# GFNet filter with a gated ReGLU branch on one core: inputs laid out by partition, idle matmuls in the head's waits, first products pass by pass, other due times

## The chip, the cores and the metric

The kernel runs on one core of one Trainium2 chip. The metric is the device time of one execution in microseconds (us); lower is better. Before the change the median of three runs is 416.8 us (415.87 to 417.68).

## The reference

The input x is 2048 rows of 512 numbers. It is normalised by row, and goes two ways: through a two-dimensional Fourier filter, and through a gated feed-forward product with a ReLU gate. The second, through SiLU, gates the first.

```python
xn = _layernorm(x, axis=-1)                       # x: (1, 2048, 512)
X  = rfft2(xn, axes=(-2, -1)) * (w_r + 1j * w_i)  # (2048, 257)
s  = irfft2(X, s=(2048, 512))
gate, up = xn @ W_gate, xn @ W_up                 # (512, 1376) each
h  = gate * (gate > 0) * up
g  = silu(h @ W_down)                             # (1376, 512)
return x + s * g
```

## The kernel before

All work on TensorE (PE) is in float16, with each float32 operand split into a high and a low half: a product is three passes, high x high, high x low and low x high (`PASSES`, line 24). High halves are mostly made by ScalarE (ACT) and low halves by VectorE (DVE), as the rest that the high half leaves.

x is worked on in 8 chunks of two row blocks (128 rows each); two chunks make one of 4 feed-forward blocks of 512 rows. A chunk `c` is loaded (`load_x`, 292), its mean and variance taken on DVE (`stats`, 305; `deviation`, 316, with one square root on ACT), normalised into `xf` (`normalise`, 357), and turned so that the model dimension lies on partitions: chunks 0 and 1 by PE transposes into `head` and from there into `xT` (`turn_row`, 399: ACT writes the high half, DVE the low half), later ones by DMA transposes. In parallel `xf` is folded and split for the Fourier stages (`fold`, `split`, `first_stage`).

The two weight matrices W_gate and W_up are cut by columns into 11 tiles of 128 (the last is 96), in seven groups (`GROUPS`, 22). `load_group` (480) loads a group's two pieces `raw`; `squares` (489, ACT) and a matmul with ones into `sum` (`group_scale`, 499) give a scale `p`; `group_split` (507) writes the high and low halves `wgu`. `product` (661) is twelve matmuls (3 passes x 4 pieces of the model dimension) into `gu`; names read `gu<block>_<tile>_<0 gate, 1 up>`. For block 0 the first three tiles are made in two halves of 256 columns, rows 0 and 1 (chunk 0) first, then rows 2 and 3 (chunk 1). `rectify` (697, ACT) makes `r` from the gate, `hidden` (703) makes `h32` (DVE) and `h16` (ACT and DVE), `down` (720) multiplies by W_down (`wds`) into `dn`, and `gate` (736) applies SiLU.

The Fourier path goes through DRAM twice: `first_stage` writes `A_d`; `fft_chunk` (767) reads it, goes through PE stages y, x, z and v, and writes `C_d`. When all of `C_d` is written, `last_stage` (927) loads `ct` in 64-partition pieces, PE makes `s2` of each chunk, ACT copies it to `zz`, GpSimd (POOL), DVE and ACT unfold it through `ae` and `ye` into `sv`, and `finish` (976) multiplies `sv` by the gate, adds it to a fresh load `xt` of x, and stores it.

The order of all work is set ahead of the run: every piece is a `step` with an engine, a cost, reads, writes and sometimes a due time; `Plan.run` (119) gives the remaining steps due times backward from these and lists the steps on each engine, earliest due first among those that could start. Due times and choices of engine are the tables of lines 33 to 41. Each engine then works its list strictly in order. `keep_busy` (391) puts matmuls on constant data into PE's list, whose result `idle` nobody reads; before the change these are 12 steps of three, all ahead of the first useful one.

DMAs are issued from SP, a few from ACT. Before the change x, W_gate, W_up, W_down and the output lie in DRAM in their natural order. Row p*32 + e*16 + n of x belongs to partition 64*e + p, so that a load of x or a store of the output is two DMAs of 64 partitions each (e = 0 and 1); a piece of W_gate is a 512-byte or 1024-byte run for each of four rows of a partition.

Every instruction is recorded through the helper in line 64, so that all rows of the profile say L64, and tiles are told apart by name.

Of the kernel before, what the change touches and what calls it, by code (L numbers as in the profile page):

```python
# [8 lines left out]
F32 = mybir.dt.float32  # L9
# [5 lines left out]
P = 128  # L15
S, D, F = 2048, 512, 1376
N1, N2 = 64, 32
# [14 lines left out]

T0, DOWN, FIRST, FIRST_STEP, MID, MID_STEP, LAST, LAST_STEP = 10.0, 56.9, 49.0, 16.8, 180.6, 14.5, 265.2, 14.8
LOADS, LOADX, LOADU = [0.5, 0.7, 3.5, None, None, None, None], [-1.2, 1.0], 4.0
FOLDS, FOLD_LEAD, MARGIN = ['DVE', 'DVE', 'DVE', 'DVE', 'DVE', 'DVE', 'DVE', 'DVE'], 18.2, 1.83
HIGH_ACT = {(0, 1), (1, 0), (1, 1), (0, 0)}
NORM, TURN1 = (('DVE', 'DVE'), ('DVE', 'ACT')), 'PE'
YCOST, VCOST, SCOST, MODE = .63, .59, .6, .095
BUSY = 12
HURRY, SLOW, SLOW_TO = -1, 1, 20  # L40
LOWS = [("DVE", "DVE")] * 8
# [10 lines left out]
def fwidth(f):  # L52
    return P if f < TAIL else F - P * TAIL
# [172 lines left out]
def pe(n, m):  # L226
    return n * (m / 2370 + .001)


@with_exitstack  # L230
def kernel(ctx: ExitStack, tc: tile.TileContext, x, wg, wu, wd, wl, ew, sp, c_r, c_d, c_m, c_x, c_s, out):
    nc = tc.nc
    PS = bass.MemoryType.PSUM
    xr, outr = (t[0].rearrange("(p e n) d -> e p n d", p=N1, n=NE) for t in (x, out))
    PE, DVE, ACT, POOL, SP = (InOrder(tc, e) for e in (nc.tensor, nc.vector, nc.scalar, nc.gpsimd, nc.sync))
# [56 lines left out]
    def load_x(c):  # L292
        tile_of(f"x{c}", "k4", [P, 2, D], F32)
        for e in range(2):
            engine, queue = (("SP", SP), ("ACT", ACT))[c == 0 and e]
            for i in range(2) if c == 0 else [None]:
                rows = slice(2 * c, 2 * c + 2) if i is None else slice(i, i + 1)
                to = slice(0, 2) if i is None else slice(i, i + 1)
                step(engine, .6, lambda e=e, queue=queue, rows=rows, to=to: queue.dma_start(T[f"x{c}"][64 * e:64 * e + 64, to], xr[e, :, rows, :]),
                     writes=[(f"x{c}", e, i)], lead=14 if c else None, kb=256 if i is None else 128, lag=2.2, due=(LOADX[c] + (i or 0) * .01) if c < 2 else None)  # L300

    def x_names(c, i):
        return [(f"x{c}", e, None if c else i) for e in range(2)]

# [86 lines left out]
    def keep_busy(n):  # L391

        tile_of("idle", "F", [P, 256], F32)
        w = ones.bitcast(F16)
        for k in range(n):
            step("PE", .43, lambda: [matmul(T["idle"], w[:, 0:P], w, start=True, stop=True) for _ in range(3)],
                 writes=["idle"], due=1. + .43 * k, lead=0.)

    def turn_row(c, i):

        if (c % 2, i) == (0, 0):
            tile_of(f"xT{c // 2}", "xg", [P, 4, 8, P], F16)
# [10 lines left out]
        step("PE", 1., run, reads=[(f"xf{c}", i), "cS"], writes=[(f"head{c}", i)])  # L413
# [66 lines left out]
    def load_group(g):  # L480
        w = sum(fwidth(f) for f in GROUPS[g])
        f0 = GROUPS[g][0] * P
        for i, src in enumerate((wg, wu)):
            tile_of(f"raw{g}_{i}", "k4", [P, 4, 2 * P], F32)
            e, queue = (("SP", SP), ("ACT", ACT))[g == 0 and i]
            step(e, .6, lambda i=i, src=src, queue=queue: queue.dma_start(T[f"raw{g}_{i}"][:, :, :w], src.rearrange("(k p) f -> p k f", p=P)[:, :, f0:f0 + w]),
                 writes=[f"raw{g}_{i}"], lead=12 if g else None, kb=2 * w, lag=2.5, due=LOADS[g])

# [75 lines left out]
    def load_down():  # L564
        n = NFT - 1
        for a, b in ((0, 3), (3, 6), (6, 8), (8, n)):
            step("SP", .6, lambda a=a, b=b: SP.dma_start(wdr[:, a + 1:b + 1, :], wd[a * P:b * P, :].rearrange("(k p) d -> p k d", p=P)),
                 writes=[("wd", f + 1) for f in range(a, b)], lead=22, kb=256 * (b - a))
        step("SP", .6, lambda: SP.dma_start(wdr[:fwidth(n), NFT, :], wd[n * P:, :]), writes=[("wd", NFT)], lead=22, kb=192)

# [90 lines left out]
    def product(c, f, i, rows=slice(0, 4), tag="gu"):  # L661
# [14 lines left out]
        def run():  # L676
# [299 lines left out]
    def finish(c, i, due):  # L976
        n, sn, g = f"xt{c}_{i}", f"sv{c}", f"g{c // 2}"
        j = 2 * (c % 2) + i
        tile_of(n, "k2", [P, D], F32)
        for e in range(2):  # L980
            step("SP", .6, lambda e=e: SP.dma_start(T[n][64 * e:64 * e + 64], xr[e, :, 2 * c + i, :]), reads=[(sn, 2)], writes=[(n, "x", e)], lead=8, kb=128)
        for part, cols in enumerate(columns(c // 2, j)):
# [3 lines left out]
            step("DVE", dve(w), lambda s=s, t=t: DVE.tensor_add(t(), t(), s()), port=True,  # L986
                 reads=[(sn, 3 + i, part), (n, "x", 0), (n, "x", 1)], writes=[(n, part)])
            for e in range(2):
                engine, queue = (("SP", SP), ("ACT", ACT))[e and c == NCH - 1 and i]
                step(engine, .6, lambda t=t, cols=cols, e=e, queue=queue: queue.dma_start(outr[e, :, 2 * c + i, cols], t()[64 * e:64 * e + 64]),  # L990
                     reads=[(n, part)], kb=w // 4, due=due, lag=2.2)

# [189 lines left out]
```

## Time and profile before

| | before |
|---|---|
| median of the runs | 416.8 us |
| lowest and highest | 415.87 and 417.68 us |
| profiled execution: span from first to last instruction | 415.5 us |
| profiled execution: other time | none is given beside the span |
| PE busy | 401.9 us, 97% of the span |
| DVE, ACT, POOL busy | 306.6, 188.3, 45.0 us |
| mean granted clock of PE | 0.985 |
| first matmul of a product (`gu`) | 12.88 us |
| end of the last matmul | 410.78 us |

The rows quoted below come from five views: the page, the waits of one engine, the chain of work that ended last in order of time, the timeline of one engine, and busy times by stretch (windows). In a timeline row stand start, time, engine, line, operation, output<-inputs, partitions x elements and count; the bracket at its end gives the engine's idle time just before, and what ended it. A window row holds the stretch, its length, busy time of the engine (and instructions), granted PE clock, busy share of the DMA engines, and GB/s.

### The profile page before, as it was taken

Reading aid. Unit: us, or ns where it says so; the run is one execution under the profiler, and the core shown is the slowest. Engines: PE = TensorE matmul, PEld = TensorE weight load, DVE = VectorE, ACT = ScalarE, POOL = GpSimd, SP = SyncE. Lnnn points to the kernel's source line nnn. Section 1 sums busy time; section 2 is a strip of 40 time slices with the busy share of each in tenths; the row PEclk is TensorE's granted clock in tenths of the full one; section 3 lists DMA queues with packets and bytes.
Section 4 is the critical chain, followed back from the end, with each engine's and each line's share of the span. In section 5 each row is a group of like instructions: output and inputs, shape, how many; then the busy total and the mean of one; then the engine's idle time right before and its main releaser. Section 6 shows DMA issues by size and latency. Waiting matters only on the chain.

```text
span 415.5 us, 7642 instructions
## 1 busy us (share of the span) xinstructions
PE 401.9 (97%) x2981; PEld 211.3 (51%) x2981; DVE 306.6 (74%) x648; ACT 188.3 (45%) x356; POOL 45.0 (11%) x68
## 2 busy tenths in 40 slices
PE   5799999999999999999999999999999999899995
PEld 4486454544444444545555455556455445444554
DVE  3758999999998897435595977888763337988943
ACT  3869863635444359320454435335414335423311
POOL 0000000000000000002030320330330018201200
PEclk9599999999999999999999999999999999999998
DMA  8992301055324777963005235053302299665614
GB/s 208 338 332 61 89 13 50 11 143 70 83 52 121 157 235 246 219 225 115 2 2 166 49 117 165 3 165 100 119 2 50 52 212 221 154 176 141 165 52 101
DMA packets 41764, 51.72 MB, mean 124 GB/s; under 512 B 16064, under 2 KB 24864, under 8 KB 41728
## 3 DMA queue, kind: packets, MB, share of 16 engines
q1 hardware_dynamic: 40880, 50.59, 45.9%
q10 hardware_dynamic: 848, 0.66, 0.6%
q8 instruction: 23, 0.38, 0.4%
q14 instruction: 13, 0.11, 0.1%
HBM read 35.48 MB, written 12.60 MB: 116 GB/s over the span
## 4 chain that ended last, share of the span: by engine, by line
PE 90%; DMA 5%; DVE 2%; SPq 1%; issue 1%; ACT 0%; DVEq 0%
PE gu L64 51%; PE dn L64 27%; PE z L64 3%; PE xx L64 3%; PE s L64 2%; DMA xt<-in_x 2%; DMA x<-in_x 2%; DMA ct<-C_d 2%; PE y L64 2%; PE v L64 2%; SPq L64 1%; PE dn_3b L64 1%; DVE wgu L64 0%; DVE xT L64 0%; DVE ye L64 0%
## 5 line engine op out<-in xcount | busy, mean ns | idle before, releaser
L64 PE MATMUL gu<-xT,wgu 128*128 128x512 f16 (+1 forms) x1032 | 217.3, 368 | 4.7 <-DVE xT L64 2.0
L64 PEld LDWEIGHTS <-wgu 128*128 128x128 f16 x1032 | 100.8, 99 | 110.6 <-issue 7.6
L64 PE MATMUL dn<-wds,h 128*128 128x512 f16 (+2 forms) x528 | 115.5, 372 | 0.0
L64 PEld LDWEIGHTS <-h 128*128 128x128 f16 (+1 forms) x561 | 53.7, 98 | 58.4 <-issue 2.5
L64 ACT ACTIVATE h<-h 128x512 f16<-128x512 f32 (+1 forms) x44 | 27.7, 629 | 70.7 <-DVE h L64 70.6
L64 DVE TENSOR_TENSOR h<-gu,r 128x512 f32<-128x512 f32 (+2 forms) x52 | 33.6, 646 | 23.3 <-PE gu L64 21.9
L64 POOL TENSOR_TENSOR po<-tt,tt 128x256 f32<-128x256 f32 x16 | 14.8, 926 | 284.3 <-DVE tt L64 236.1
L64 ACT ACTIVATE r<-gu 128x512 f32<-128x512 f32 (+1 forms) x44 | 26.1, 593 | 24.6 <-PE gu L64 24.3
L64 DVE TENSOR_TENSOR h<-h,h 128x512 f16<-128x512 f32 (+1 forms) x44 | 30.0, 690 | 4.5 <-ACT h L64 4.2
L64 POOL TENSOR_TENSOR ae<-zz 128x128 f32<-128x128 f32 (+1 forms) x32 | 18.6, 613 | 61.9 <-ACT zz L64 48.5
L64 DVE SCALAR_TENSOR_TENSOR tt<-xsp,cw,wt 128x512 f32<-128x512 f32 x32 | 25.2, 849 | 0.0
L64 ACT ACTIVATE g<-dn,cdi 128x512 f32<-128x512 f32 (+1 forms) x16 | 10.6, 673 | 25.2 <-PE dn L64 25.1
L64 DVE TENSOR_TENSOR z<-z,z 128x1024 f16<-128x1024 f32 x8 | 9.8, 1222 | 15.4 <-ACT z L64 15.4
L64 DVE TENSOR_TENSOR sv<-sv,g 128x512 f32<-128x512 f32 (+1 forms) x17 | 10.9, 673 | 9.7 <-ACT g L64 9.0
L64 DVE BATCH_NORM_STATS2 st<-x 128x6 f32<-128x512 f32 x16 | 10.9, 683 | 8.3 <-DMA x<-in_x 8.3
L64 PE MATMUL gu<-xT,wgt 128*64 128x256 f16 (+1 forms) x144 | 17.0, 309 | 0.0
L64 DVE TENSOR_TENSOR a<-y,a 128x1024 f16<-128x1024 f32 x8 | 9.7, 1218 | 8.0 <-ACT a L64 8.0
L64 ACT ACTIVATE wgu<-raw 128x512 f16<-128x512 f32 x20 | 12.4, 622 | 6.3 <-DMA raw<-in_wu 6.3
L64 DVE SCALAR_TENSOR_TENSOR wgu<-raw,p,wgu 128x512 f16<-128x512 f32 x20 | 14.5, 746 | 0.5 <-ACT wgu L64 0.4
L64 DVE TENSOR_TENSOR xt<-xt,sv 128x512 f32<-128x512 f32 (+1 forms) x17 | 11.5, 690 | 4.4 <-DMA xt<-in_x 4.4
L64 ACT ACTIVATE xs<-xs 128x1024 f16<-128x1024 f32 x8 | 8.5, 1059 | 12.4 <-DVE xs L64 12.4
L64 PEld LDWEIGHTS <-wgt 128*64 128x64 f16 (+1 forms) x144 | 9.5, 106 | 7.1 <-issue 1.7
(135 smaller groups left out, 423.4 us busy)
## 6 DMA issues: line engine op xcount, KB each, us to landing
A_d<-t SPq DMA_DIRECT2D x16, 256.0 KB, 3.2
rw<-in_wl SPq DMA_DIRECT2D x8, 512.0 KB, 6.0
wt<-in_wl SPq DMA_DIRECT2D x8, 512.0 KB, 4.8
at<-A_d SPq DMA_DIRECT2D x8, 512.0 KB, 4.8
C_d<-t SPq DMA_DIRECT2D x16, 256.0 KB, 3.3
ct<-C_d SPq DMA_DIRECT2D x16, 256.0 KB, 6.4
xt<-in_x SPq DMA_DIRECT2D x32, 128.0 KB, 2.8
out<-xt SPq DMA_DIRECT2D x30, 128.0 KB, 2.3
```

The lines of the kernel that those rows point to most:

```text
L64: return lambda *args, **kw: self.tc.keep_in_program_order(f(*args, **kw))
```

## The change

Five things are changed together; what is computed stays the same.

1. **Layout.** The host hands x over as (128 partitions, 16 row blocks, 512), both weight matrices as one array `w` in which each group's gate piece and up piece are contiguous for each partition, and W_down by partition (with its tail of 96 rows as an array of its own). The output is written in the layout of x, and the host puts it back in order. Loads of x and stores of the output become one DMA of 128 partitions where there were two of 64; weight pieces become one run of 2 KB or 4 KB for each partition.
2. **Queues at the start.** Both pieces of group 0 are issued from ACT, and all of x from SP; before, ACT issued half of chunk 0 and the up piece of group 0.
3. **Idle matmuls.** `BUSY` goes from 12 steps to 60: 9 of three matmuls and 51 of one, with a late due time, so that the planner can put them between useful steps.
4. **First products.** The half products of tile 0 for rows 0 and 1 are issued pass by pass (4 matmuls each, with due times 0.9 us apart), and those of all split tiles run over the pieces within a pass, not over the passes within a piece. A step waits for the halves that it reads.
5. **Tables.** Other due times, loads in another order, both normalisations of chunk 0 on ACT, other high halves on ACT.

```diff
-T0, DOWN, FIRST, FIRST_STEP, MID, MID_STEP, LAST, LAST_STEP = 10.0, 56.9, 49.0, 16.8, 180.6, 14.5, 265.2, 14.8
+T0, DOWN, FIRST, FIRST_STEP, MID, MID_STEP, LAST, LAST_STEP = 5.52, 50.66, 44.31, 17.14, 179.63, 14.68, 274.73, 15.17
...
-HIGH_ACT = {(0, 1), (1, 0), (1, 1), (0, 0)}
-NORM, TURN1 = (('DVE', 'DVE'), ('DVE', 'ACT')), 'PE'
+HIGH_ACT = {(0, 1), (2, 1), (0, 0), (1, 0), (1, 1), (3, 0)}
+NORM, TURN1 = (('ACT', 'ACT'), ('ACT', 'DVE')), 'PE'
...
-BUSY = 12
+BUSY, BUSY_COLD = 60, 9
...
     def load_x(c):
         tile_of(f"x{c}", "k4", [P, 2, D], F32)
-        for e in range(2):
-            engine, queue = (("SP", SP), ("ACT", ACT))[c == 0 and e]
-            for i in range(2) if c == 0 else [None]:
...
-                step(engine, .6, lambda e=e, queue=queue, rows=rows, to=to: queue.dma_start(T[f"x{c}"][64 * e:64 * e + 64, to], xr[e, :, rows, :]),
...
+            step("SP", .6, lambda rows=rows, to=to: SP.dma_start(T[f"x{c}"][:, to], x[:, rows, :]),
...
     def keep_busy(n):
...
-            step("PE", .43, lambda: [matmul(T["idle"], w[:, 0:P], w, start=True, stop=True) for _ in range(3)],
-                 writes=["idle"], due=1. + .43 * k, lead=0.)
+            m = 3 if k < BUSY_COLD else 1
+            at = .43 * min(k, BUSY_COLD) + .11 * max(k - BUSY_COLD, 0)
+            step("PE", (.43, .11)[m == 1], lambda m=m: [matmul(T["idle"], w[:, 0:P], w, start=True, stop=True) for _ in range(m)],
+                 writes=["idle"], due=90., lead=90. - at)
...
     def load_group(g):
...
-            e, queue = (("SP", SP), ("ACT", ACT))[g == 0 and i]
-            step(e, .6, lambda i=i, src=src, queue=queue: queue.dma_start(T[f"raw{g}_{i}"][:, :, :w], src.rearrange("(k p) f -> p k f", p=P)[:, :, f0:f0 + w]),
...
+            e, queue = (("SP", SP), ("ACT", ACT))[g == 0]
+            step(e, .6, lambda i=i, queue=queue: queue.dma_start(T[f"raw{g}_{i}"].rearrange("p k f -> p (k f)"), w_in[:, 8 * f0 + 4 * i * w:8 * f0 + 4 * i * w + 4 * w]),
...
     def product(c, f, i, rows=slice(0, 4), tag="gu"):
...
+        def part(n):
+            h, l = PASSES[n]
+            t, xT = T[name][:, i] if tag == "F" else T[name], T[f"xT{c}"]
+            for k in range(4):
+                matmul(t[:, rows], wgu[g][:, h, i, k, o:o + P], xT[:, rows, l * 4 + k, :], start=k == n == 0, stop=k == 3 and n == 2)
...
+        if len(r) < 4:
+            if rows.start == 0 and f == 0:
+                for n, (h, l) in enumerate(PASSES):
+                    step("PE", pe(4, 256), lambda n=n: part(n), reads=[(f"xT{c}", j, l) for j in r] + [("wgu", f, h, i)], writes=out, due=clock[0] + n * .9)
+                tick(pe(12, 256))
+            else:
+                cost = pe(12, 256)
+                step("PE", cost, lambda: [part(n) for n in range(3)], reads=[(f"xT{c}", j, h) for j in r for h in range(2)] + weights(f, i), writes=out, due=tick(cost))
+            return
...
     def finish(c, i, due):
...
-        for e in range(2):
-            step("SP", .6, lambda e=e: SP.dma_start(T[n][64 * e:64 * e + 64], xr[e, :, 2 * c + i, :]), reads=[(sn, 2)], writes=[(n, "x", e)], lead=8, kb=128)
+        step("SP", .6, lambda: SP.dma_start(T[n], x[:, 2 * c + i, :]), reads=[(sn, 2)], writes=[(n, "x")], lead=8, kb=256)
...
-            for e in range(2):
-                engine, queue = (("SP", SP), ("ACT", ACT))[e and c == NCH - 1 and i]
...
+            step("SP", .6, lambda t=t, cols=cols: SP.dma_start(out[:, 2 * c + i, cols], t()), reads=[(n, part)], kb=w // 2, due=due, lag=2.2)
```

What the planner makes of this is seen in the order of the instructions. PE's list around the first products, before (`sum0` and `sum1` are the scale matmuls of groups 0 and 1, `head0` the transposes of chunk 0):

```order
L64 MATMUL idle_111<-ones_93 128x256
L64 MATMUL sum0_188<-m0_173,ones_93 128x2
L64 MATMUL head0_196<-cS_75,xf0_190 128x128 x8
L64 MATMUL sum1_217<-m1_186,ones_93 128x2
L64 LDWEIGHTS wgu0_76
L64 MATMUL gu0_0_0_229<-xT0_214,wgu0_76 128x256
```

and in the changed kernel, from the end of the idle matmuls behind `sum1` to the first product:

```order
L64 MATMUL idle_111<-ones_93 128x256
L64 MATMUL head0_248<-cS_75,xf0_234 128x128 x4
L64 LDWEIGHTS ones_93
L64 MATMUL idle_111<-ones_93 128x256
L64 MATMUL head0_248<-cS_75,xf0_234 128x128 x4
...
L64 LDWEIGHTS wgu0_76
L64 MATMUL gu0_0_0_273<-xT0_264,wgu0_76 128x256
```

In the changed kernel 46 idle matmuls stand ahead of `sum0`, 20 between `sum0` and `sum1`, 9 between `sum1` and the transposes, one between the two rows' transposes and two behind them; before, 36 stand ahead of `sum0` and none behind. The product's first four matmuls are followed there by four of the up half and then by eight more of the gate half.

ACT's list in the same place, before:

```order
L64 ACTIVATE wgu0_76,m0_173<-raw0_1_126 128x512
L64 ACTIVATE q0_171<-q0_171 128x2
L64 ACTIVATE wgu0_76,m0_173<-raw0_0_131 128x512
L64 ACTIVATE wgu1_77,m1_186<-raw1_0_139 128x512
L64 ACTIVATE wgu1_77,m1_186<-raw1_1_144 128x512
L64 ACTIVATE wgu0_76<-raw0_0_131,p0_201 128x512
L64 ACTIVATE xT0_214<-head0_196 128x512 x2
```

and in the changed kernel (rows with `m0` or `m1` are squares, those with `p0` high halves, `q0` is the square root):

```order
L64 ACTIVATE wgu0_76,m0_154<-raw0_0_115 128x512
L64 ACTIVATE wgu0_76,m0_154<-raw0_1_122 128x512
L64 ACTIVATE wgu1_77,m1_195<-raw1_0_131 128x512
L64 ACTIVATE q0_206<-q0_206 128x2
L64 ACTIVATE wgu1_77,m1_195<-raw1_1_139 128x512
L64 ACTIVATE wgu0_76<-raw0_0_115,p0_197 128x512
L64 ACTIVATE xf0_234<-x0_120,q0_206 128x512 x2
L64 ACTIVATE wgu0_76<-raw0_1_122,p0_197 128x512
L64 ACTIVATE xT0_264<-head0_248 128x512 x2
```

Group 0's squares now come first, and the two normalisations of chunk 0 (`xf0`) are in ACT's list where they were in DVE's.

Far behind, in the last Fourier stage, ACT's list puts `r3_5` (which frees the PSUM of product `gu3_5_0`) behind the copy into `sv1` before:

```order
L64 ACTIVATE ye3_4235<-zz3_4214 128x2
L64 ACTIVATE zz4_4237<-s2_4_4187,cwi_88 128x1024
L64 ACTIVATE ae4_4257<-zz4_4237 128x2 x2
L64 ACTIVATE ye4_4260<-zz4_4237 128x2
L64 ACTIVATE sv1_4264<-ye1_4143 128x4
L64 ACTIVATE r3_5_4266<-gu3_5_0_4216 128x512
L64 ACTIVATE h16_3_4_4270<-h32_3_4_4185 128x512
```

and in the changed kernel ahead of it:

```order
L64 ACTIVATE ye2_4227<-zz2_4194 128x2
L64 ACTIVATE r3_5_4229<-gu3_5_0_4169 128x512
L64 ACTIVATE zz3_4245<-s2_3_4198,cwi_88 128x1024
L64 ACTIVATE ae3_4250<-zz3_4245 128x2 x2
L64 ACTIVATE ye3_4254<-zz3_4245 128x2
L64 ACTIVATE h16_3_4_4257<-h32_3_4_4162 128x512
L64 ACTIVATE ye1_4192<-ae1_4189 128x2
L64 ACTIVATE sv1_4279<-ye1_4192 128x4
```

The copy into `sv1` needs `ye1` from DVE, where `ye1` stands in both kernels behind the two additions into `xt0_0` and `xt0_1`. On SP the loads of `xt0` stand in both kernels behind twelve loads of `ct`; they are four DMAs before and two now.

More of the change, by code (lines that the diff above doesn't have):

```diff
@@ L230, with kernel @@
 @with_exitstack
-def kernel(ctx: ExitStack, tc: tile.TileContext, x, wg, wu, wd, wl, ew, sp, c_r, c_d, c_m, c_x, c_s, out):
+def kernel(ctx: ExitStack, tc: tile.TileContext, x, w_in, wd, wd_tail, wl, ew, sp, c_r, c_d, c_m, c_x, c_s, out):
     nc = tc.nc
     PS = bass.MemoryType.PSUM
-    xr, outr = (t[0].rearrange("(p e n) d -> e p n d", p=N1, n=NE) for t in (x, out))
     PE, DVE, ACT, POOL, SP = (InOrder(tc, e) for e in (nc.tensor, nc.vector, nc.scalar, nc.gpsimd, nc.sync))
@@ L293, in load_x @@
         tile_of(f"x{c}", "k4", [P, 2, D], F32)
[L294 to L300 removed]
+        for i in range(2) if c == 0 else [None]:
+            rows = slice(2 * c, 2 * c + 2) if i is None else slice(i, i + 1)
+            to = slice(0, 2) if i is None else slice(i, i + 1)
+            step("SP", .6, lambda rows=rows, to=to: SP.dma_start(T[f"x{c}"][:, to], x[:, rows, :]),
+                 writes=[(f"x{c}", i)], lead=14 if c else None, kb=512 if i is None else 256, lag=2.2, due=(LOADX[c] + (i or 0) * .01) if c < 2 else None)
     def x_names(c, i):
[L303 removed]
+        return [(f"x{c}", None if c else i)]
     def stats(c, q, j):
@@ L412, in run @@
                 PE.transpose(head()[:, cols], T[f"xf{c}"][:, i, cols], cS[:, 7:])
-        step("PE", 1., run, reads=[(f"xf{c}", i), "cS"], writes=[(f"head{c}", i)])
+        step("PE", .5, run, reads=[(f"xf{c}", i), "cS"], writes=[(f"head{c}", i)])
         step("ACT", act(512), lambda: ACT.activation(xt(0), head(), AF.Copy), reads=[(f"head{c}", i)], writes=[(f"xT{c // 2}", j, 0)])
@@ L482, in load_group @@
         f0 = GROUPS[g][0] * P
-        for i, src in enumerate((wg, wu)):
-            tile_of(f"raw{g}_{i}", "k4", [P, 4, 2 * P], F32)
-            e, queue = (("SP", SP), ("ACT", ACT))[g == 0 and i]
-            step(e, .6, lambda i=i, src=src, queue=queue: queue.dma_start(T[f"raw{g}_{i}"][:, :, :w], src.rearrange("(k p) f -> p k f", p=P)[:, :, f0:f0 + w]),
-                 writes=[f"raw{g}_{i}"], lead=12 if g else None, kb=2 * w, lag=2.5, due=LOADS[g])
+        for i in range(2):
+            tile_of(f"raw{g}_{i}", "k4", [P, 4, w], F32)
+            e, queue = (("SP", SP), ("ACT", ACT))[g == 0]
+            step(e, .6, lambda i=i, queue=queue: queue.dma_start(T[f"raw{g}_{i}"].rearrange("p k f -> p (k f)"), w_in[:, 8 * f0 + 4 * i * w:8 * f0 + 4 * i * w + 4 * w]),
+                 writes=[f"raw{g}_{i}"], lead=12 if g else None, kb=2 * w, lag=2.2, due=LOADS[g])
     def squares(g):
@@ L690, in run @@
                     n += 1
-        r = range(*rows.indices(4))
+        def part(n):
[3 more added lines that the diff above has]
+                matmul(t[:, rows], wgu[g][:, h, i, k, o:o + P], xT[:, rows, l * 4 + k, :], start=k == n == 0, stop=k == 3 and n == 2)
+        r = range(*rows.indices(4))
+        out = [(name, j // 2, i) for j in r if j % 2 == 0]
+        sums[c, f, i] = (lambda: T[name][:, i] if tag == "F" else T[name]), [(name, k, i) for k in range(2)]
+        if len(r) < 4:
[7 more added lines that the diff above has]
+            return
         cost = 1.33 if f == TAIL and i == 1 else pe(12, 128 * len(r))
         step("PE", cost, run, mode=3 * (f == TAIL and i == 1), reads=[(f"xT{c}", j, h) for j in r for h in range(2)] + weights(f, i),
-             writes=[(name, j // 2, i) for j in r if j % 2 == 0], due=tick(cost))
-        sums[c, f, i] = (lambda: T[name][:, i] if tag == "F" else T[name]), [(name, k, i) for k in range(2)]
+             writes=out, due=tick(cost))
     def rectify(c, f):
@@ L986, in finish @@
             step("DVE", dve(w), lambda s=s, t=t: DVE.tensor_add(t(), t(), s()), port=True,
[L987 to L991 removed]
+                 reads=[(sn, 3 + i, part), (n, "x")], writes=[(n, part)])
+            step("SP", .6, lambda t=t, cols=cols: SP.dma_start(out[:, 2 * c + i, cols], t()), reads=[(n, part)], kb=w // 2, due=due, lag=2.2)
     step("SP", .6, lambda: SP.dma_start(cR, c_r), writes=["cR"], lead=20, kb=256)
```

21 lines of the change are left out of this document (13 added, 8 removed).

## The prediction

> **What bounds the kernel now.** First the page: who is busy, and the granted clock in 40 slices.
>
> ```profile
> span 415.5 us, 7642 instructions
> PE 401.9 (97%) x2981; PEld 211.3 (51%) x2981; DVE 306.6 (74%) x648; ACT 188.3 (45%) x356; POOL 45.0 (11%) x68
> PEclk9599999999999999999999999999999999999998
> ```
>
> PE is busy for 97% of the span, and the change takes no useful matmul away. So it can only gain where PE waits or runs at a low clock; the second slice, about 10 to 21 us, is the only long one at half clock. Next PE's waits:
>
> ```profile
> PE sum L64 <- ACT wgu L64: 2.7, 1, 2.7
> PE gu L64 <- DVE xT L64: 2.0, 1, 2.0
> PE gu L64 <- ACT r L64: 1.6, 1, 1.6
> ```
>
> The first two lie ahead of the products or in the first. The chain in order of time tells why, and where the third stands (start, length, what):
>
> ```profile
> 4.86 7.45 DMA x<-in_x
> 12.40 0.70 DVE st L64
> 13.89 1.30 DVE xT L64 x2
> 15.23 6.74 PE gu L64 x35
> 23.14 1.46 DVE wgu L64 x3
> 24.65 7.91 PE gu L64 x70
> ...
> 343.89 7.71 DMA xt<-in_x
> 354.61 2.75 PE gu L64 x12
> ...
> 410.80 0.48 ACT g L64
> ```
>
> The second chunk of x, 7.45 us on its way, holds the statistics on DVE, and these stand in DVE's list ahead of the low halves of `xT`, for which PE waits until 15.23. Then 35 matmuls take 6.74 us, 193 ns each; from 24.65 on 70 take 7.91, 113 ns each. From there PE waits once, for 1.6 us before 354.61, for `r` on ACT, which stands behind work that hangs on the loads `xt`. From 354.61 nothing but PE is on the chain until the last SiLU.
>
> The clock, by stretches that fit its steps (PE busy, granted clock, DMA share, GB/s):
>
> ```profile
> 1.05:3.84 2.79, 2.79 (x14) 1.00 0.60 160
> 3.84:6.50 2.66, 2.66 (x24) 1.00 0.95 223
> ...
> 7.25:10.67 3.42, 1.05 (x8) 1.00 1.12 274
> ...
> 14.08:17.49 3.41, 2.26 (x11) 0.50 1.07 365
> 17.49:20.91 3.42, 3.42 (x18) 0.50 1.06 377
> 20.91:24.32 3.41, 3.41 (x34) 1.00 1.08 364
> ```
>
> (For 1.05 to 3.84 no grant is recorded yet; 199 ns for each of the idle matmuls, against 111 ns behind 3.84, says it was half.) The clock is lost at the end of a stretch with PE busy 1.05 of 3.42 us, and comes back only after a stretch filled completely.
>
> **The change, part by part.**
>
> *Loads.* Rates of stretches in which nearly all packets are of one kind, 512-byte pieces of weights first, then 2 KB rows of W_down; and DVE's wait for the first row of x:
>
> ```profile
> 6.50:9.00 2.50, 1.00 1.16 314
> 17.00:19.00 2.00, 0.50 1.04 386
> ...
> 4.47 0.69 DVE L64 BATCH_NORM_STATS2 st<-x 128x6 f32<-128x512 f32 x1 [3.46 <-DMA x<-in_x]
> 7.77 0.63 ACT L64 ACTIVATE wgu<-raw 128x512 f16<-128x512 f32 x1 [5.54 <-DMA raw<-in_wu]
> ```
>
> Now the first 1 MB is group 0 and both rows of chunk 0 (four DMAs of 256 KB, two from each queue). One row has landed by 4.47 before; the other 0.79 MB take 2.0 to 2.5 us at 386 to 314 GB/s, so all have landed by 6.5 to 7.0, where the first weight piece landed at 7.77 before. [...]
>
> *Scale of group 0.* A square takes 0.63 (row above) and up to 0.8 with the read-out of its sum, so the last is done between 7.3 and 7.8. But `sum0` now queues behind 46 idle matmuls: 14 by 3.84, 32 at 111 ns, to 7.4. So `sum0` stands at about 7.6; before:
>
> ```profile
> 9.25 0.38 PE L64 MATMUL sum<-m,ones 128*128 128x2 f32 x2 [2.74 <-ACT wgu L64]
> 10.00 1.43 PE L64 MATMUL head<-cS,xf 128*128 128x128 f32 x8 [0.37 <-DVE xf L64]
> 23.26 1.04 PE L64 MATMUL head<-cS,xf 128*128 128x128 f32 x8
> ```
>
> *From there to the first product.* These rows price the steps: DVE's scale of a group, the deviation with its square root on ACT between, ACT's normalisation, both high halves of `xT`:
>
> ```profile
> 22.12 0.16 DVE L64 TENSOR_SCALAR p<-sum 128x2 f32<-128x2 f32 x1 [2.48 <-PE sum L64]
> 22.32 0.37 DVE L64 TENSOR_SCALAR p<-p 128x2 int32<-128x2 int32 x2
> 17.70 0.17 DVE L64 TENSOR_SCALAR q<-mv 128x2 f32<-128x2 f32 x1
> 19.21 0.16 DVE L64 SCALAR_TENSOR_TENSOR q<-mv,q 128x2 f32<-128x2 f32 x1
> 19.40 0.82 ACT L64 ACTIVATE xf<-x,q 128x512 f32<-128x512 f32 x1
> 11.77 1.06 ACT L64 ACTIVATE xT<-head 128x512 f16<-128x512 f32 x2
> ```
>
> `sum0` 7.6, done 8.0; scale 0.6 to 8.6; deviation 1.67 (17.70 to 19.37) to 10.3, since `q0` now queues behind `p0` on DVE; two normalisations on ACT, the first done at 11.1, the second at 11.9 (before, DVE did both while ACT made squares); ACT's other high half, at the square's 0.63, to 12.5; high halves of `xT` 1.06 to 13.5. PE starts there. Its first eight matmuls need high halves alone (0.9 us). The low halves follow on DVE, which first does `p1` (`sum1`, behind 20 idle matmuls, at 10.2; 0.3 and 0.6 to 11.2), a low half of weights (0.7) and both statistics of chunk 1 (0.70 and 0.2 each; its load, now one DMA of 128 partitions on a faster stream, no longer holds them), to 13.8. Two low halves at 1.30: 15.1 to 15.2.
>
> So PE runs on from 15.2, as before from 15.23, but with 8 of the first 48 matmuls done and at full clock. The other 40 take 4.5 us at 113 ns, the `sum2` among them 0.3, the transposes 1.04: the third product starts at 21.0. Before it started at 24.65. **Gain 3.6 us**, of it some 2.3 from the clock (29 matmuls from 15.23 to 20.91, 80 ns each), the rest from the eight matmuls done early and the wait for `wgu` from 24.3 (23.26 and 1.04) to 24.65. That wait may come back: `sum2` stands behind 24 of the matmuls, at 17.9, `p2` at 18.2; from there to the last split DVE took 2.5 us before (22.12 to 24.6), so 20.7. The margin is 0.3; without it at most the 0.4 of before is lost.
>
> *Idle matmuls and the clock's phase.* When the clock is released is not in the kernel's hands: 2.8 us after PE began in one place, 5.7 in the other (15.23 to 20.91). If it comes 3.4 us later, 17 more idle matmuls cost 88 ns each ahead of `sum0`: between 0 and 1.5 us lost. I take the middle, **0.8 us back**. The idle matmuls between `sum0`, `sum1` and the transposes (20 and 9, 2.2 and 1.0 us) end about when their successors are ready, and cost nothing.
>
> *Late wait.* DVE and SP there:
>
> ```profile
> 349.50 0.72 DVE L64 TENSOR_TENSOR xt<-xt,sv 128x512 f32<-128x512 f32 x1 [0.92 <-DMA xt<-in_x]
> 351.72 0.97 DVE L64 TENSOR_TENSOR xt<-xt,sv 128x512 f32<-128x512 f32 x1 [1.50 <-DMA xt<-in_x]
> 332.05 7.78 SPq L64 DMA_DIRECT2D ct<-C_d x12
> 340.46 3.89 SPq L64 DMA_DIRECT2D xt<-in_x x4
> ```
>
> Behind twelve `ct` loads SP issues four `xt` loads 1.1 us apart (340.46 to the chain's 343.89), since each waits for an earlier DMA; two are left, so that the second row is issued some 2.2 us earlier and `xt0_1` is added by about 350.3 instead of 352.4 (times of before). Also `r3_5` no longer queues behind `sv1`. What is late next: `h32_3_5` on DVE, behind `xt0_1` and two halves of `ye1`; by the 0.72 for 512 columns about 1.4 us later, 351.7. PE came to its wait at 353.0 (354.61 less 1.6) and comes to this one no earlier. So **1.6 us gained**; between 0 and 1.6 if the loads don't come sooner.
>
> *Hidden.* Twice fewer `x`, `xt` and `out` DMAs on SP: SP is waited for nowhere else. A PE that runs 3.6 us ahead needs splits and folds sooner: DVE's and ACT's own waits for loads (3.46 and 5.54 us in the rows above, and the chain's 7.45) shrink with it; if they did not, up to 3.6 would be given back. The tail behind PE, 4.7 us from 410.78 to the end of the span, keeps its steps; its last store is one DMA instead of two on two queues, which I cost at nothing.
>
> **Sum.** -3.6 + 0.8 - 1.6 = -4.4 us on the span of 415.5: 411.1. The median of the runs lies 1.3 above that span, and I keep that: **412.4 us**.
>
> **Rivals.**
>
> *The clock falls anyway in the head.* Between the last long run of idle matmuls and 15.2 PE does 8 transposes, 3 idle matmuls and 8 of the product: some 2.2 of 3.4 us. At 1.05 of 3.42 the clock was lost, at 2.26 of 3.41 it was not given back. If it falls, the 2.3 go: 414.7. For it: that gap in the evidence; against: the idle matmuls run right up to the transposes. [...] Chance 0.10.
>
> *A wait takes the place of the late one*, since DVE's list there is as full as before: 1.6 stays, 414.0. Chance 0.12.
>
> *Slower: the additions of x bind the last stage.*
>
> ```profile
> 354.60:372.50 17.90, 16.23 (x30) 1.00 0.71 183
> DMA to landing us min/median/max: 2.2/2.6/8.4
> ```
>
> DVE is 91% busy there (first row), some 0.65 us spare for a chunk of about 7 (two products at the chain's 2.75, a down step and an `s2`). On SP the `xt` loads of a chunk now stand behind both stores of the chunk before, so they are issued only when DVE has done it. DVE has about 4.3 us of other work until it needs them (four instructions of 512 columns at 0.72 and four of half the width), the loads two or three issues and 2.6 us (second row, median). If landing took 2 us longer, five chunks would lose some 1.3 each, 6.5 in all, and the kernel ends at 418.9; that is the point from which it is slower. For it: 8.4 as the longest; against: that was behind twelve `ct` loads, and a load is now one DMA of 128 partitions. Chance 0.05.
>
> *It doesn't do what it says*: idle matmuls hold up `sum0` by as much as the loads gain, and no late gain: -3.6 + 1.5 + 0.4 = -1.7, 415.1. Chance 0.06.
>
> **Numbers.** About 0.5%, 2.1 us, is what a measurement can tell from no change: faster is below 414.7, slower above 418.9. My forecast, 411 to 414, has 0.67, and with the 0.12 of the late wait and a share of the borders 0.81 for faster; 0.14 for the same (first and last rival, less that share), 0.05 for slower. The range holds the forecast, the late wait and both rivals near 415: 410.6 (1.0 better in the head, no phase cost) to 415.3.
>
> **What would show it.** Right: granted clock 1.00 without a gap from about 4 us; first `gu` at 13 to 14.5; the third product near 21; no wait of PE of 1 us from there to the end. Wrong: half clock in 10 to 21; `sum0` after 9; PE waits for ACT `r` or DVE `h` near 350; DVE waits for `xt` chunk after chunk.

## The result, and the profile after

| | before | changed |
|---|---|---|
| median of four runs (lowest to highest) | 417.24 us (415.87 to 418.29) | **410.87 us** (410.83 to 410.96) |
| profiled execution's span | 415.5 us | 409.1 us (its run took 410.83) |
| mean granted clock | 0.985 | 0.997 |
| third product starts | 24.65 us | 20.05 us |
| span less that start | 390.85 us | 389.05 us |

The changed kernel takes 0.9844 of the time before (95% interval 0.9817 to 0.9871), 6.4 us less. It was run again beside the experiments, and there it gave 411.4 us; why those two differ is part of what follows.

The page of the changed kernel, first the busy times and then the clock:

```profile
span 409.1 us, 7662 instructions
PE 402.5 (98%) x3023; PEld 213.4 (52%) x3023; DVE 306.6 (75%) x646; ACT 190.0 (46%) x359; POOL 47.6 (12%) x68
PEclk9999999999999999999999999999999999999998
```

The slice at half clock is gone, and PE is busy 98% of a shorter span. The whole list of PE's waits:

```profile
PE idle L64 <- DVE md L64: 1.1, 1, 1.1
PE gu L64 <- ACT xT L64: 1.0, 1, 1.0
PE gu L64 <- DVE xT L64: 0.3, 1, 0.3
```

The waits for `sum` (2.7 us before) and for `r` (1.6) are no longer there. PE's timeline in the head:

```profile
1.05 6.69 PE L64 MATMUL idle<-ones 128*128 128x256 f16 x46 [1.05 <-DVE md L64]
7.58 0.28 PE L64 MATMUL sum<-m,ones 128*128 128x2 f32 x2
...
13.35 1.03 PE L64 MATMUL gu<-xT,wgu 128*128 128x256 f16 x8 [0.96 <-ACT xT L64]
14.67 2.78 PE L64 MATMUL gu<-xT,wgu 128*128 128x256 f16 x24 [0.29 <-DVE xT L64]
...
19.17 1.04 PE L64 MATMUL head<-cS,xf 128*128 128x128 f32 x8
20.05 2.13 PE L64 MATMUL gu<-xT,wgu 128*128 128x256 f16 x18
```

`sum0` stands right behind the idle matmuls, the eight high-half matmuls run at 13.35, the low halves come at 14.67, and the third product (last row) starts at 20.05. Before, the chain in order of time began with SP's issues (0.73 to 4.81) and the load of `x` behind them (4.86, 7.45 us). Now its first long piece is this:

```profile
1.05 6.69 PE idle L64 x46
```

The idle matmuls themselves now begin the chain, so they have become a part of what sets the end. The load of chunk 1 no longer does: SP issues it at 3.07 as one DMA, where the first of its two halves went out at 4.30 behind six other issues, and DVE takes the statistics of its first row without a wait (before, at 12.40, behind a wait for the load):

```profile
11.38 0.69 DVE L64 BATCH_NORM_STATS2 st<-x 128x6 f32<-128x512 f32 x1
```

In the table the gain splits at the third product: 4.6 us ahead of it, 1.8 behind it, together 6.4. Behind it, the late wait's 1.6 and 0.4 of the tail (4.7 us from the last SiLU at 410.80 to the end before, 4.3 from 404.83 now) make 2.0; some 0.2 was lost elsewhere.

The clock, by stretches that fit its steps (PE busy, granted clock, DMA share, GB/s):

```profile
4.15:7.56 3.41, 3.41 (x33) 1.00 1.03 368
7.56:10.98 3.42, 3.42 (x35) 1.00 1.03 403
10.98:14.39 3.41, 2.44 (x21) 1.00 1.04 425
```

In the trace full clock is granted at 4.15 us, and from there to the tail it is never lost, the window with PE's wait in it (2.44 of 3.41) included. The DMAs move 368 to 425 GB/s in these windows; before they moved 274 to 377 in the windows from 7.25 to 24.32.

That the part behind the head is nearly constant makes the experiments easy to read: in the eight profiles of the changed kernel and its variants in which PE waits nowhere behind the head, span less start of the third product comes out at 388.9 to 389.1, so a kernel's head can be read from one row.

### The profile page after: what moved, and what is told of

It is laid out like the page before. It is cut to its first block, busy times and chain, and to the rows that moved or that the text cites. A ratio compares the mean times of both kernels' runs of the same rounds, so it can differ in the third digit from the quotient of the medians.

```text
span 409.1 us, 7662 instructions
## 1 busy us (share of the span) xinstructions
PE 402.5 (98%) x3023; PEld 213.4 (52%) x3023; DVE 306.6 (75%) x646; ACT 190.0 (46%) x359; POOL 47.6 (12%) x68
## 4 chain that ended last, share of the span: by engine, by line
PE 98%; DVE 0%; ACT 0%; issue 0%
PE gu L64 55%; PE dn L64 27%; PE s L64 3%; PE z L64 3%; PE xx L64 3%; PE idle L64 2%; PE y L64 2%; PE v L64 2%; PE dn_3b L64 1%; PE head L64 0%; ACT xT L64 0%; PE sum L64 0%; DVE xT L64 0%; ACT g L64 0%; DVE sv L64 0%
## 5 line engine op out<-in xcount | busy, mean ns | idle before, releaser
L64 PE MATMUL gu<-xT,wgu 128*128 128x512 f16 (+1 forms) x1032 | 214.8, 364 | 1.2 <-ACT xT L64 1.0
L64 PEld LDWEIGHTS <-wgu 128*128 128x128 f16 x1032 | 99.4, 98 | 105.0 <-issue 4.6
L64 POOL TENSOR_TENSOR ae<-zz 128x128 f32<-128x128 f32 (+1 forms) x32 | 21.3, 698 | 62.5 <-ACT zz L64 43.2
L64 DVE TENSOR_TENSOR sv<-sv,g 128x512 f32<-128x512 f32 (+1 forms) x17 | 11.8, 722 | 7.5 <-ACT g L64 6.9
```

The costliest lines, as they stand in the source:

```text
L64: return lambda *args, **kw: self.tc.keep_in_program_order(f(*args, **kw))
```

## The experiments

All but two keep the order of every engine as it was, and edit what one step issues; so a difference belongs to the edit. Times are medians of four to twelve runs, on four chips. The kernel before ran beside each of them and took 416.76 to 417.23 us, so a difference of half a microsecond between runs on different chips is not told from none. The ratios in brackets are to before on the same chip, with their 95% intervals.

**The changed kernel again.**

> The changed kernel once more, as the measure for the others. Its first four runs lay at 410.8 to 411.0 us, with the 46 idle matmuls done in 6.69 us; in the runs that differ only behind the head or in the weights' pieces they took 7.28 and 7.31 us and the time was 411.5 to 411.7 us. If the moment at which the clock comes is chance: 410.8 to 411.8 us here, and the span is 389.0 us more than the start of the third product. If the 0.6 us were the price of those edits: 410.9 us again.

411.40 us (410.64 to 412.12). In its profile the 46 idle matmuls take 7.38 us and everything up to the third product (20.74) shifts with them; span 409.7, less 20.74 gives 388.96:

```profile
1.05 7.38 PE L64 MATMUL idle<-ones 128*128 128x256 f16 x46 [1.05 <-DVE md L64]
8.27 0.28 PE L64 MATMUL sum<-m,ones 128*128 128x2 f32 x2
...
20.74 5.51 PE L64 MATMUL gu<-xT,wgu 128*128 128x256 f16 x49
```

So it is chance: the five runs here, all on one chip, reach from below the first four to 1.2 us above them. In the traces full clock is granted at 4.15 us in the first profile of the changed kernel, at 5.57 here, and anywhere from 3.78 to 7.04 in the others, a spread of 3.3 us, about one window of 3.41 us. Here 1.42 us later cost 0.69. The first four runs, which differ by 0.13 us, were probably all early ones (only one of them left a trace), and 411.4 is the better measure for what follows.

**Idle matmuls alone, in the kernel before.**

```diff
+            if g == 0:
+                idle(24)
             matmul(T[f"sum{g}"][:, :2 * nf], ones, T[f"m{g}"][:, :2 * nf], start=True, stop=True)
+            if g < 2:
+                idle((3, 9)[g])
...
+                    if (c, f, i, n) == (0, 0, 0, 1) and rows.start == 0:
+                        idle(20)
```

> The kernel before, every instruction in its old place, with 56 idle matmuls put into PE's waits of the head (24 ahead of sum0, 3 behind it, 9 behind sum1, 20 behind the first matmul of the first product). If the clock is the main part of the head's gain: granted clock 1.00 from about 4 us on, the 35 matmuls from 15.2 take about 4.0 us instead of 6.7, and of these 2.7 us all but the 0.4 of the wait for wgu stays: about 414.5 us, with runs closer together than 415.9 to 418.3. If the gain lies in the layout and the loads: no change, 416 to 418 us.

415.01 us (ratio 0.9941, 0.9921 to 0.9961): 2.2 us faster, and the clock stays. The 35 matmuls of the first product:

```profile
15.53 3.98 PE L64 MATMUL gu<-xT,wgu 128*128 128x256 f16 x35
```

3.98 us against 6.74. The nine runs lie within 2.2 us (413.92 to 416.11), the twenty of before beside them within 4.7 (415.34 to 420.07). So they are closer together, as was expected, though they are fewer; the 2.2 us that are left come from something else than losing the clock. PE's late wait for `r`, in the old order and with loads in halves, is only 0.45 us here (ahead of the product at 351.20).

**The changed kernel without the added idle matmuls.**

```diff
-BUSY, BUSY_COLD = 60, 9
+BUSY, BUSY_COLD = 12, 12
```

> The changed kernel with the 36 idle matmuls of before and no others; the order of all else is the same. If the clock is the main part: it is lost near 10 us and comes back only after a stretch filled by PE, some 20 to 35 matmuls at 80 ns more, 2 to 3 us; sum0 comes about 0.9 us earlier since no idle matmul stands ahead of it: 412.0 to 413.2 us. If the layout is the main part: 410.0 us, the 0.9 gained and nothing lost.

411.95 us (0.9863, 0.9832 to 0.9893), just below the first expectation, and only 0.5 above the changed kernel's second measurement, the control from here on. The two ranges overlap (411.42 to 412.77 and 410.64 to 412.12) and the chips differ, so the 0.5 is not shown by itself. PE by clock window:

```profile
5.99:9.40 3.41, 1.83 (x18) 1.00 1.03 401
9.40:12.82 3.42, 1.54 (x10) 1.00 1.04 417
12.82:16.23 3.41, 3.13 (x15) 0.50 1.01 413
16.23:19.64 3.41, 3.41 (x34) 1.00 1.03 417
```

The clock is lost after a window with PE busy 1.54 of 3.42 us, but comes back after one window, not three as before, since the products now fill it. That window holds 15 matmuls where full ones hold 33 to 35: the price is about 1.4 us (15 at 96 ns more than the 113 of a full one), and `sum0`, with fewer idle matmuls ahead of it (7.39, against 8.27 in the control), returns 0.9. In the new order the idle matmuls are worth little, some 0.5 us by these numbers.

**Layout alone, in the kernel before**, as in the change's layout hunks, with the old tables, product and idle matmuls:

```diff
-queue.dma_start(T[f"x{c}"][64 * e:64 * e + 64, to], xr[e, :, rows, :])
+None if e else queue.dma_start(T[f"x{c}"][:, to], x[:, rows, :])
...
-SP.dma_start(T[n][64 * e:64 * e + 64], xr[e, :, 2 * c + i, :])
+None if e else SP.dma_start(T[n], x[:, 2 * c + i, :])
```

> The kernel before with x, weights, W_down and result laid out by partition, x, xt and out each as one DMA of 128 partitions; the order of every engine, the product and the idle matmuls are those of before. If layout and clock add up to the whole (clock alone brought 2.2 us in this order): about 4 us faster than before, 413 us, with the late wait of PE gone and the first product about 1.5 us earlier, and half clock in a part of the head. If the layout works only together with the new order, which asks for its loads at other times: 415 us or more, with the late wait still there.

413.61 us (0.9913, 0.9890 to 0.9936): 3.6 us faster. The six runs fall into two groups, 412.26 to 412.94 and 414.28 to 414.41, and the profile is one of the second. All of `x` is issued from SP here, as in the change. PE gets its low halves at 13.04, 2.2 us sooner than the kernel before and 1.6 sooner than the changed one. The clock is lost from 11.98 to 18.81. And the late wait is there, though each `xt` is one DMA:

```profile
13.04 6.79 PE L64 MATMUL gu<-xT,wgu 128*128 128x256 f16 x35 [1.11 <-DVE xT L64]
...
352.08 2.75 PE L64 MATMUL gu<-xT,wgu 128*128 128x512 f16 x12 [1.19 <-ACT r L64]
```

**Layout and idle matmuls, in the kernel before** (`idle(8)` ahead of `sum0`, 3 and 14 behind `sum0` and `sum1`, 10 behind the first matmul, added to the last one).

> The kernel before with the new layout (as in the run with layout alone) and 35 idle matmuls in PE's waits of the head; order, due times and product are those of before. If clock and layout add up: the 35 matmuls from 13.0 take 4.0 instead of 6.8 us, the third product starts near 20, the late wait of 0.4 to 1.2 us stays: 411.0 to 412.3 us, so that of the change's 6.3 us only about 1 is left for the new order and the passes. If the new order is needed for the head (the splits of group 2 late on DVE): third product after 21, 412.5 us or more.

411.82 us (0.9877, 0.9855 to 0.9898), with 411.40 for the changed kernel on the same chip. Its head is the shorter one, even with the clock as late as 7.04; the late wait gives that back:

```profile
12.98 3.98 PE L64 MATMUL gu<-xT,wgu 128*128 128x256 f16 x35
...
19.13 7.11 PE L64 MATMUL gu<-xT,wgu 128*128 128x256 f16 x60
...
349.74 2.75 PE L64 MATMUL gu<-xT,wgu 128*128 128x512 f16 x12 [1.51 <-ACT r L64]
```

So layout and idle matmuls make 4.9 of the 5.4 us seen on this chip; new tables and passes add 0.4, which is less than the control's own spread and not shown by these medians. By the profiles, they lose 1.6 in the head (20.74 less 19.13) and gain 2.0 behind it (390.97 less 388.96).

**Weights in 512-byte pieces (1 KB for groups of two tiles), in the changed kernel.**

```diff
-queue.dma_start(T[f"raw{g}_{i}"].rearrange("p k f -> p (k f)"), w_in[:, 8 * f0 + 4 * i * w:8 * f0 + 4 * i * w + 4 * w])
+queue.dma_start(T[f"raw{g}_{i}"], (wg, wu)[i].rearrange("(k p) f -> p k f", p=P)[:, :, f0:f0 + w])
```

> The changed kernel with the gate and up weights read from their old place in pieces of 512 bytes (1 KB for the groups of two); x stays laid out by partition and the order is the same. If pieces of 512 bytes cost rate (314 against 386 GB/s in the trace of before): the weights of groups 0 and 1 land 0.3 to 0.8 us later; the first lie under the idle matmuls ahead of sum0, the second hold ACT's squares ahead of the normalisation, so the first product starts about 0.5 us later: 411.4 us. If pieces of 512 bytes run at full rate: 410.9 us.

411.53 us, the same as the control. The rate is lower, 320 against 420 GB/s from 9 to 12 us (the run without the added idle matmuls, on the same chip as this one, shows 417 from 9.40 to 12.82), and ACT's first two squares start 1.05 and 1.2 us later. Window and ACT's rows in this kernel:

```profile
9.00:12.00 3.00, 3.00 (x31) 1.00 1.15 320
```

```profile
5.36 0.63 ACT L64 ACTIVATE wgu<-raw 128x512 f16<-128x512 f32 x1 [3.14 <-DMA raw<-in_wg]
6.88 0.63 ACT L64 ACTIVATE wgu<-raw 128x512 f16<-128x512 f32 x1 [0.79 <-DMA raw<-in_wu]
```

and in the control:

```profile
9.00:12.00 3.00, 3.00 (x31) 1.00 1.05 420
```

```profile
4.31 0.63 ACT L64 ACTIVATE wgu<-raw 128x512 f16<-128x512 f32 x1 [2.08 <-DMA raw<-in_w]
5.67 0.63 ACT L64 ACTIVATE wgu<-raw 128x512 f16<-128x512 f32 x1 [0.64 <-DMA raw<-in_w]
```

But `sum0` stands behind the idle matmuls until 8.2 anyway. In the changed kernel the weights' layout is hidden under them; what the layout brings there is x's part.

**All x transfers in halves, in the changed kernel.**

```diff
-SP.dma_start(T[n], x[:, 2 * c + i, :])
+[SP.dma_start(T[n][e:e + 64], x[e:e + 64, 2 * c + i, :]) for e in (0, 64)]
```

and likewise for the loads of `x` and the stores.

> The changed kernel with every x, xt and out transfer as two DMAs of 64 partitions each on the same queue, in the same order. If the late wait went because the xt loads are fewer DMAs and so issued sooner: a wait of PE of 1 to 1.6 us near 350 is back, and the rows of x land later in the head, 0.3 to 1 us on the first product: 412.5 to 413.5 us. If it went because r3_5 no longer stands behind the work that waits for xt: no wait near 350, and at most 0.5 us in the head: 411.0 to 411.4 us.

416.08 us (0.9970, 0.9949 to 0.9991): nearly all of the gain is gone, beyond both expectations. The third product starts at 21.29, and span less that is 392.9: 3.9 us are lost behind the head. PE has no wait near 350; its waits lie further on in the last stage. PE's rows there:

```profile
381.06 1.04 PE L64 MATMUL dn<-wds,h 128*128 128x512 f16 x4 [1.21 <-DVE h L64]
382.86 1.50 PE L64 MATMUL gu<-xT,wgt 128*64 128x256 f16 x24 [0.76 <-DVE h L64]
388.65 4.01 PE L64 MATMUL dn<-wds,h 128*128 128x512 f16 x16 [0.38 <-DVE h L64]
```

These three make 2.35 of the 3.9. Some 0.8 more lies in the same stretch, where weight loads wait for `h` too (0.88, 0.53 and 0.49 us from 388.65 to 390.33), and 0.7 in the tail: from the last SiLU (409.23) to the end are 4.97 us, against 4.27 in the changed kernel. DVE's waits for `xt` (us in total, times, longest):

```profile
DVE xt L64 <- DMA xt<-in_x: 5.2, 7, 2.1
```

and SP's rows of one chunk:

```profile
357.13 2.43 SPq L64 DMA_DIRECT2D out<-xt  x4
359.62 2.51 SPq L64 DMA_DIRECT2D xt<-in_x  x4
```

SP's two rows of a chunk in the changed kernel:

```profile
355.40 0.94 SPq L64 DMA_DIRECT2D out<-xt  x2
356.47 0.89 SPq L64 DMA_DIRECT2D xt<-in_x  x2
```

Eight issues of some 0.6 us each keep SP 4.9 us per chunk, four of some 0.45 keep it 1.8. DVE then waits for `xt` (2.3 us and once in the changed kernel), falls behind, and PE waits for `h`.

**Only the late loads, and only the stores, in halves.**

> The changed kernel with only the late xt loads as two DMAs of 64 partitions each; x in the head and the stores stay whole. With everything in halves the kernel took 416.1 us, 1.2 us of it in the head and some 3.9 in the last stage, where DVE waited for xt chunk after chunk. If that comes from the number of issues that stand on SP ahead of a load (four xt of 0.62 us, behind four stores of 0.60): half the surplus goes with the stores, about 1.2 us of 2.4 in a chunk, and with some 0.7 us spare in a chunk little is left: 411.0 to 412.5 us. If it comes from loads of 64 partitions being slow in themselves: 414 us or more.

411.68 us: span 409.7 less 20.67 is 389.03, so nothing is lost behind the head, and no late wait.

> The changed kernel with only the stores as two DMAs of 64 partitions each. With loads and stores in halves the last stage lost 3.9 us, with the loads alone in halves nothing. If it is the number of issues on SP between one chunk's stores and the next chunk's loads (eight in halves 4.9 us; four stores and two loads about 3.3 us, less than the 3.6 us of two stores and four loads that lost nothing): no wait of PE behind the head, the span 389.0 us more than the start of the third product, 410.6 to 411.8 us. If a store in halves is itself the slow part: PE waits for h in the last stage, 413 us or more.

413.55 us (412.74 to 414.88): the second case came out, not the first. Span 411.0 less 19.87 is 391.1, 2.1 lost. Half lies behind PE: from the last SiLU (405.68) to the end are 5.3 us, 1.05 more than in the changed kernel. Of this, 0.8 is the last store, whose two issues keep SP for 1.11 us where one took 0.33. The other half lies on PE, of which one row shows 0.38; behind it weight loads wait for `h` (0.53 and 0.49 us, at 385.96 and 386.78):

```profile
385.11 4.01 PE L64 MATMUL dn<-wds,h 128*128 128x512 f16 x16 [0.38 <-DVE h L64]
```

So it isn't the count of issues alone: this kernel has no more than the one before it. DVE now waits 0.38 and 0.32 us for the second row of two chunks. The stores stand ahead of the loads in SP's list, but that doesn't explain it: counted from the start of the third product, the loads of the first of these chunks have all been issued by 332.4 us here, and by 332.9 in the run before, where DVE doesn't wait for them. Why they come late here stays open. The loss with both in halves, 3.9, is more than the 0 and 2.1 of each alone; that DVE's slack can be used up only once would fit, but is not shown.

**First products not pass by pass.**

```diff
-lambda n=n: part(n)
+lambda n=n: [part(m) for m in range(3)] if n == 2 else None
```

> The changed kernel with the first two products not taken pass by pass: the twelve matmuls of each stand together where its third pass stood; the order of all else is the same. PE then waits from 12.4 for the low halves at 14.6 and starts 8 matmuls of 0.11 us later than they could: 0.9 us, 411.8 us. If the 2.2 us in which PE does nothing cost the clock as well, some 2 us more: 413 to 414 us.

411.99 us; from `sum0` to the third product 12.90 us against 12.47 in the control: the passes are worth 0.43 by the profiles, half of what was expected; the medians, on different chips, can't tell it. The gate half's four high-half matmuls still ran early; only the up half's four moved. The clock stayed (34 matmuls fill the 3.41 us from 15.98).

**Nine idle matmuls fewer ahead of `sum0`** (the steps of `keep_busy` with `k` from 9 to 17 issue nothing).

> The changed kernel with 37 idle matmuls ahead of sum0 instead of 46, all else in its order. sum0 stood at 7.58 while its squares were done at 6.4. If sum0 and the scale behind it set the first product: sum0 at 6.6, the first product 0.9 us earlier, 410.0 us. If ACT's own list does (a square of group 1 that waits for its load at 7.67 stands ahead of the square root, another and a split ahead of the normalisation): at most 0.2 us, 410.7 us; and should the clock be lost in the longer gap, 412 us.

410.96 us (410.28 to 411.27). `sum0` at 7.33 and the first product at 13.20:

```profile
7.33 0.38 PE L64 MATMUL sum<-m,ones 128*128 128x2 f32 x2 [0.17 <-ACT wgu L64]
...
13.20 1.03 PE L64 MATMUL gu<-xT,wgu 128*128 128x256 f16 x8 [0.95 <-ACT xT L64]
```

From `sum0` to the first product are 5.87 us here, and 5.77 in the changed kernel and the control. So the first product moves with `sum0`: the chain behind it did set the head. The gain is small here, since the squares were only ready at 7.3 in this profile, and 0.4 between medians of two chips is not shown by itself.

**The deviation ahead of the scale.** In DVE's and ACT's lists nine steps were moved by hand, so that chunk 0's deviation and normalisation no longer stand behind `sum0`, and 15 idle matmuls were left out:

```diff
+        move = {68: 6.75, 69: 6.76, 70: 6.8, 71: 7.8, 72: 7.82, 74: 8.9, 75: 8.95, 95: 11.39, 97: 12.45}
+        order = [(move.get(s.order, t), s) for t, s in order]
         order.sort(key=lambda k: k[0])
```

> The changed kernel with the head's order on DVE and ACT mended by hand: the deviation of x's first chunk goes ahead of the scale of group 0 on DVE (it no longer waits for sum0), its square root ahead of the squares of group 1 on ACT, the normalisation ahead of the split of group 0, the statistics of chunk 1 ahead of the scale of group 1; 15 idle matmuls fewer. If the scale behind sum0, and so the idle matmuls ahead of it, set the first product: the first product at 12.3 instead of 13.35, the third near 18.9 instead of 20.05, and 389.0 behind it: 409.7 us, and less spread, since sum0 has slack. If DVE, which from 7.2 to 20.5 has hardly an idle stretch, binds the splits of group 2: the third product waits, 410.5 us or more; if the clock is lost between the shorter runs of idle matmuls: 412 us.

**410.13 us** (409.61 to 410.33), and 0.9834 (0.9812 to 0.9856) of before; all its runs lie below all five of the control (410.64 to 412.12). It beats both kernels. The new order and the idle matmuls left out were not tried apart. The clock came late (6.47 us), `sum0` stood at 8.71, and still:

```profile
8.71 0.28 PE L64 MATMUL sum<-m,ones 128*128 128x2 f32 x2
...
12.86 4.10 PE L64 MATMUL gu<-xT,wgu 128*128 128x256 f16 x32 [0.95 <-ACT xT L64]
...
19.56 6.71 PE L64 MATMUL gu<-xT,wgu 128*128 128x256 f16 x60
```

The low halves no longer hold PE at all. The third product starts 1.2 us before the control's, 0.7 short of the expected 18.9; x's second row and the up weights came later in this profile than in the first (DVE's statistics of that row start at 6.98 against 6.32, ACT's square of those weights at 6.77 against 5.67).

## Why the prediction was right, and where it was not

The direction, the range and the main mechanism held: 412.4 was forecast, 410.87 and 411.4 were measured. The first lies just below the 411 to 414 that were given the most weight, the second in it. The head was to give 2.8 us (3.6 less 0.8); it gave 4.6 in the first profile, 3.9 in the control's. Point by point:

- *Loads, `sum0`, first product* (6.5 to 7.0, 7.6, 13.5): all landed by 6.3, 7.58, 13.35. Right. The lower rate of 512-byte pieces, which the prediction read from the trace of before (314 against 386 GB/s), shows again in the experiment (320 against 420), but it made no difference to the time: the prediction itself put `sum0` behind the idle matmuls, and should have seen that weights landing 1 us later would be free.
- *Low halves at 15.1 to 15.2, third product at 21.0*: 14.67 and 20.05. The term "gain 3.6 us" was mis-sized. Two sums were too long. Ahead of the low halves, short steps overlap where I had put them end to end: `sum1` stood at 9.90, not 10.2, and `p1` was done by 10.71, not 11.2. And from the low halves to the third product I added 4.5, 0.3 and 1.04 to 5.8; between the starts of the rows it is 5.4 (14.67 to 20.05), because a group's busy time in the profile holds the end of its last matmul, under which the next group begins (the row at 14.67 ends at 17.45, and the next one starts at 17.29).
- *Clock*: kept, as forecast. Its share "some 2.3" is about the 2.2 that the idle matmuls alone bring in the old order, and the 1.8 that they bring there on top of the layout (413.61 to 411.82, two chips). In the new order they are worth only some 0.5, if that, as the run without them shows: with the new layout and order the products themselves bring the clock back two windows sooner (after 3.41 us there, from 12.82 to 16.23; after 10.24 before, from 10.67 to 20.91). So the clock is not what carries this change; the layout is (3.6 alone).
- *The clock's phase*, 0.8 back: nothing in the first runs, 0.7 in the control's profile. About right as a mean; the first runs were at the lucky end.
- *Late wait*, 1.6 gained: the wait did go, but the reason was wrong, and that the size came out is in part luck, since in the old order this wait is 0.45, 1.19, 1.51 and 1.57 us in four profiles. "The second row is issued some 2.2 us earlier" is not what removes it: in the changed kernel DVE still waits 2.29 us for `xt` there and has added both rows by 350.04, where the forecast, moved by the head's 4.6, would have been 345.7; and PE passes without a wait. (The 352.4 for before should read 352.7, from 351.72 and 0.97.) With whole loads in the old order the wait stays (1.19 and 1.51), with halved loads in the new order it is gone. So what counts is the new order. The prediction gave one part of it in half a sentence, `r3_5` ahead of `sv1` on ACT, and the traces show it: before, the copy into `sv` waits for DVE, and `r` stands right behind it; in the changed kernel `r` is made 6.3 us ahead of that copy. On PE a step of `down` (350.34, 1.46 us) also stands ahead of the next product now (351.63), while DVE makes the `h` at 350.63; before, such a step came only behind the product that waited (357.19). Neither was tried by itself. DVE's row of the additions and ACT's two rows in the changed kernel:

```profile
348.22 1.82 DVE L64 TENSOR_TENSOR xt<-xt,sv 128x512 f32<-128x512 f32 x2 [2.29 <-DMA xt<-in_x]
344.46 0.60 ACT L64 ACTIVATE r<-gu 128x512 f32<-128x512 f32 x1 [0.30 <-PE gu L64]
350.74 0.21 ACT L64 ACTIVATE sv<-ye 128x4 f32<-128x4 f32 x1 [3.32 <-DVE ye L64]
```

and ACT's two rows before:

```profile
353.86 0.21 ACT L64 ACTIVATE sv<-ye 128x4 f32<-128x4 f32 x1 [3.75 <-DVE ye L64]
353.98 0.58 ACT L64 ACTIVATE r<-gu 128x512 f32<-128x512 f32 x1
```

- *Tail*, costed at nothing: 0.4 gained.
- *Hidden*: "SP is waited for nowhere else" overlooked the head, where the chain before begins with SP's issues ahead of the load of chunk 1; with fewer DMAs that load is issued at 3.07, not at 4.30.
- *From span to run*: the 1.3 that was added is too small. Every run with a span on record lies 1.7 to 2.0 above it; the 415.5 of before belongs to a run above the median.
- *The slower rival*, x's additions binding the last stage: it did not happen, but its mechanism is real. With all of x's transfers in halves in the new order, 3.9 us are lost behind the head, 0.7 of them in the tail, instead of the 6.5 that I put on it. Order and layout belong together there.
- *The clock falls in the head*: not in any run with the added idle matmuls. Of the bounds 7.25, 10.67, 14.08, 17.49 and 20.91 of the prediction's stretches, only 10.67 and 20.91 are changes of the clock; the changes in the trace of before, at 3.84, 10.67 and 20.91, lie 6.83 and 10.24 us apart, two and three times 3.41.

## What to carry to other kernels

When the work behind a point is bound by one engine, take the start of that point as the measure: here span less start of the third product was the same to 0.1 us in eight profiles, and each edit could be read from one row. Count DMA issues on the queue that a late load stands in: two halves cost twice the issues, here some 0.6 us each against some 0.45 for a whole one. The stores belong to the count too, since halving them alone cost 2.1 us. Filler work that keeps a clock up (worth 2.2 us in the old order here, at most some 0.5 in the new one) should not stand ahead of a short step that starts a chain, and a chain should not hang on that step if it doesn't need its result.

## What the runs showed of the hardware

- When the clock is granted is spread over 3.78 (stores alone in halves) to 7.04 us (layout and idle matmuls) from profile to profile, though PE starts at 1.05 in nearly all of them.
- It was lost after windows in which PE was busy 1.05 (before), 1.51 (layout alone) and 1.54 of some 3.4 us (without the added idle matmuls), and kept after 1.73 (first products not pass by pass) and 1.83 (again without the added ones). At half clock, a window with 2.36 (layout alone) did not bring it back, one with 3.13 (without the added ones) did. In the windows that lost it, transposes were most of PE's work (some 0.7, 1.1 and 1.4 us), in the one of 1.73 only some 0.2; these runs don't separate the kind of work from the busy time. Two windows of the run with the layout alone, then that of 1.73 and the one behind it:

```profile
8.57:11.98 3.41, 1.51 (x11) 1.00 1.03 408
11.98:15.40 3.42, 2.36 (x12) 0.50 1.03 427
```

```profile
12.57:15.98 3.41, 1.73 (x15) 1.00 1.03 419
15.98:19.39 3.41, 3.41 (x34) 1.00 1.00 404
```

- An issue of a DMA of 128 partitions kept SP some 0.45 us in the last stage (0.89 for two loads), one of 64 partitions some 0.6 (2.51 for four), each with the gap behind it.
